# Fused attention and two mixtures on one core: the second mixture's 2 MB loads two steps later, the first long list's tokens one step later, the last gates' operations behind the last denominators

## The chip, the cores and the metric

The kernel runs on 1 core of one Trainium2 chip. A time is the device time of one execution in microseconds (us). Before the change three runs gave 623.2, 625.92 and 627.24 us, so the median is 625.92 us. One more execution was taken by the profiler: 622.31 us, of which the trace covers a span of 620.5 us from the first to the last instruction. All rows below come from that execution, and their start times are us from the span's start.

The engines are named as in the profile: PE is the matmul engine (PEld its weight loads), DVE the vector engine, ACT the scalar engine, POOL the general engine, SP the engine that issues most of the transfers (SPq is its queue).

## The reference

Three layers follow each other, in 32-bit floats.

```
attention: 2 batches x 8 heads, 768 tokens, head width 64; keys and queries are assigned
           to one of 16 clusters of their head, and a query sees the keys of its cluster
           scores = q.k / 8 with a mask; softmax; times v        -> x, 1536 tokens x 512
mixture 1: logits = x@w_gate + log1p(exp(x@w_noise)) * noise     (8 experts)
           top 2 experts of each token, softmax over the two
           out[token] += weight * (relu(x@w1[e]) @ w2[e])        w1 512x1024, w2 1024x512
mixture 2: logits = x@phi (32 slots, 4 per expert)
           slot_input = softmax over tokens(logits).T @ x
           slot_out   = relu(slot_input @ w1[e]) @ w2[e]
           out        = softmax over slots(logits) @ slot_out
```

## The kernel before, in words

**Attention.** Pairs of heads are worked on one after the other; a pair has 12 units of scores, so the table of things to do runs over units, and `LAST` = 84 is the first unit of the last pair. Each half of a pair ends with its denominators (`den`: PE sums, a transpose `dt` and a reciprocal `rd` on DVE) and with `xout`, which writes the tokens' rows `x` and the parts of the gates' logits `gp`.

**Gates.** The first mixture's routing is made in three pieces of 6, 3 and 3 chunks of 128 tokens (`Dispatch.gate`). A piece is a list of some 40 short operations, on DVE mostly (line L690 is the helper that issues them); it has one call of `rank`, which is six small operations on PE (tile `prank`, L736 to L739) that wait for the piece's two-hot matrix `mb`. At the end stand the scatters of 128 rows each into the lists `xg`, on POOL (L757). The list `todo` holds all these operations with the unit from which each may be issued, and `gap(s, n)` takes up to n of them where the kernel's code calls it. So the numbers in `mix`, `lead` and `quota` set where the operations stand between other work on every engine. `LEAD[1]` is how many of the second piece's operations may go from unit 96, ahead of the last denominators; the others go from 99. `lead` says how many are issued around the first call of `M1.first`, `quota` how many before and after `M1.second` in steps 0 to 3. Some names in the rows are reused rooms: the third piece's tiles are cut out of `xr`.

**First mixture.** There are ten lists of tokens (jobs): two short ones of 256 rows (half the tokens of experts 0 and 1), six long ones of 448 down to 384 rows (experts 2 to 7, sorted by size at run time, `perm`), and two short ones again. Each list takes 8 steps, one for each 128 of the 1024 hidden columns: steps 0 to 15 are the first two lists, 16 to 63 the long ones, 64 to 79 the last two. In step s the kernel issues `first(s+1)` (12 matmuls into `ph`, L1054; then H on ACT, L1059, and its remainder on DVE, L1060), `second(s)` (matmuls into `py`, L1094 for short and L1121 for long lists) and the split of weights for step s+3 into a high part (ACT, L952) and a low part (DVE, L959). `load_w(s+5)` loads 512 KB of weights into one of four rooms `wr` (L946, L948), which the low part of step s+1 sets free.

**Tokens of a list.** `load_x(j)` loads a list's rows (`xr`, L975, four transfers) and its weights and row numbers (`mt`, L987, L989) on SP. For the first long list it stands behind `load_perm`, which reads six expert numbers into SP's registers (L938); the step is `LX`. For the other long lists it stands in the second step of the list before. The rows are transposed on DVE (`prep_t`, L1009) from the third step of that list on, copied on ACT (L1016), and the low part is made on DVE or POOL (L1022). A finished long list is turned back by 16 transposes on DVE (L1130), scaled on ACT, and added to the result `x2acc` in DRAM by POOL's indirect transfers (L1144).

**Second mixture.** Its weights come in halves of 2 MB (`M2.load_w`, L1205, tile `v`). Six of them go at the steps in the table `V1`, all on SP's queue, in between the first mixture's loads. They are used in the second mixture only.

What fixes the order is the order of the code: each engine executes its own instructions in the order in which they were issued, and SP its transfers.

Of the kernel before, what the change touches and what calls it, by code (L numbers as in the profile page):

```python
# [52 lines left out]
PH, PL = 1, 1  # L53
JX, JT, JN = 4, (10, 2), 2
SC = -9, -8, -7, -6, -5, -4, -3, -2, -1, 0, 1, 2
LEAD = 1, 16
SP = 1, 2, 3, 4, 6, 8
SL, MX = 1, 94
LT = (8, 9), (6, 6)
# [8 lines left out]

UN = (0,) + (10,) * 9 + (9,) * 4
SLOTS = {0: (0, 0, 2, 2, 1, 2, 2), 9: (0, 2, 1, 1, 2, 1, 2), 10: (0, 2, 1, 2, 1, 2, 2)}  # L70
V1 = 32, 36, 40, 44, 48, 58
TURN = 3, 4, 3, 3, 3, 4, 0, 0
LAST = 12 * (NP - 1)

# [400 lines left out]
class Dispatch:  # L475
# [68 lines left out]
    def gate0(self, n):  # L544
# [6 lines left out]
        def t(name, *shape, dt=F32):  # L551
            if name not in T:
                m = 1
                for x in shape:
                    m *= x
                names = " ".join("abc"[:len(shape)])
                a = g.place(m) if dt is F32 else g.place(m // 2).bitcast(dt)
                T[name] = a.rearrange(f"p ({names}) -> p {names}", **dict(zip("abc", shape)))
            return T[name]
# [7 lines left out]
        PL, PW = (lambda i=i: self.pg[:, 8 * n * i:8 * n * i + 8 * n].rearrange("p (c e) -> p c e", e=E) for i in range(2))  # L567
        M0, M1, V0, V1, TT, SS = (lambda k=k: t(k, n) for k in ("m0", "m1", "v0", "v1", "tt", "ss"))
        MB = lambda: t("mb", n, E, dt=BF16)
# [5 lines left out]
        def op(f, *a, **k):  # L575
            out.append(lambda: f(*[x() if callable(x) else x for x in a], **k))
# [38 lines left out]
        op(TTn, PW, PW, bce(self.iode), op=OP.mult)  # L615
        top(V1, PW)
        op(TTn, oh[1], PW, lambda: bcn(V1()), op=OP.is_equal)
        op(PT, MB, oh[0], oh[1], op=OP.add)
# [879 lines left out]
def body(tc, qk, q2, k2, v2, cent, wgn, noise, w12, phi, v12, out):  # L1498
    nc = tc.nc
    with ExitStack() as ctx:  # L1500
# [152 lines left out]
        for i in range(Dp.NFILL):  # L1653
            at(ends, 2 * (i // 4) + 3, Dp.fill, i)

        LX = 8
        todo = []
        gates = [Dp.gate(q, *x) for q, x in enumerate(((0, 6), (6, 3), (9, 3)))]

        def mix(s, ops, rows, every):  # L1660

            rows = list(rows)
            for i, f in enumerate(ops):
                todo.append((s, f))
                if rows and i % every == every - 1:
                    todo.append((s, rows.pop(0)))
            todo.extend((s, f) for f in rows)
# [8 lines left out]
        n1, n2 = at_rank(a), at_rank(z)  # L1676
        mix(MX, a[:LEAD[0]], [], 1)
        mix(96, a[LEAD[0]:LEAD[1]], [], 1)
        x, y = a[n1 + 1:], z[9:n2]
        turns = a[LEAD[1]:n1] + z[:9] + a[n1:n1 + 1]  # L1680
        while x:
# [4 lines left out]
        mix(99, z[n2:], [], 1)  # L1686
        mix(99, [], gates[2][1], 1)
        half = len(todo) - half
        quota = {0: (19, 9), 1: (9, 0), 2: (14, 14), 3: (14, 14)}
        lead = n1 - LEAD[1] + 1, 4  # L1690

        def gap(s, n):
            while n > 0 and todo and todo[0][0] <= s:
# [126 lines left out]
        for s in range(ns):  # L1820
            j, f = M1.steps[s]
            if 4 + len(SP) <= s + 5 < ns:
                M1.load_w(s + 5)
            if s == LX:
                while todo:
# [46 lines left out]
            if s == X9:  # L1872
                M1.load_x(9)
            if s in V1:
                M2.load_w()
# [78 lines left out]
```

## Time and profile before

| | before |
|---|---|
| runs (us) | 623.2, 625.92, 627.24 |
| profiled execution (us) | 622.31 |
| its span (us) | 620.5 |
| PE busy | 598.1 us, 96% |
| DVE busy | 426.2 us, 69% |
| ACT busy | 323.0 us, 52% |
| POOL busy | 288.3 us, 46% |
| granted PE clock, mean | 0.997 |
| moved by transfers | 139.50 MB, 225 GB/s over the span |

A row of the timeline gives the start, the duration, the engine, the line, the operation, the tiles (written <- read), how many were merged, and in brackets how long the engine was idle just before and what ended that. Shares of busy time are of little use here, since PE is nearly always busy: what matters is where PE has gaps, and which engine or transfer ended each of them.

### The profile page before, as it was taken

What the parts mean: (1) busy time and instruction counts of PE and PEld (TensorE: products, weight loads), DVE (VectorE), ACT (ScalarE), POOL (GpSimd) and SP (SyncE); (2) the same over time, 40 slices, a digit from 0 to 9 for tenths busy, and PEclk for the clock granted to TensorE, in tenths of its full rate; (3) what the DMA queues carried; (4) which work ended last, traced back from release to release, by engine and by line L of the source; (5) the groups of instructions that cost most, each with busy time, mean ns of one, the idle gap of its engine ahead of it and who ended that gap; (6) DMA issues with size and microseconds to landing.
All of it is one profiled execution on the core that took longest, in us unless ns stands there. A gap on an engine that the chain in (4) does not pass through costs nothing. (4 is left out here: it accounts for less than half of the span.)

```text
span 620.5 us, 11580 instructions
## 1 busy us (share of the span) xinstructions
PE 598.1 (96%) x4215; PEld 482.7 (78%) x4215; DVE 426.2 (69%) x854; ACT 323.0 (52%) x470; POOL 288.3 (46%) x266
## 2 busy tenths in 40 slices
PE   8999999999999998999999999999989999988996
PEld 6666767666677766878999999999989988875544
DVE  6875787676776498757455949878675877646633
ACT  5877667676676571545344463545536365533002
POOL 3998778787989851643030250513306034220100
PEclk9999999999999999999999999999989999999999
DMA  8262475552347684897835479798986979988995
GB/s 311 87 233 68 159 277 190 184 188 107 129 173 256 233 242 157 270 246 189 198 102 127 144 205 269 264 295 311 291 187 141 261 234 331 318 282 308 425 396 205
DMA packets 59116, 139.50 MB, mean 225 GB/s; under 512 B 11504, under 2 KB 27056, under 8 KB 57008
## 3 DMA queue, kind: packets, MB, share of 16 engines
q1 hardware_dynamic: 53168, 125.31, 59.9%
q0 software_dynamic: 5888, 13.42, 10.4%
q8 instruction: 34, 0.56, 0.4%
q14 instruction: 26, 0.21, 0.1%
HBM read 108.18 MB, written 28.42 MB: 220 GB/s over the span
## 5 line engine op out<-in xcount | busy, mean ns | idle before, releaser
L959 DVE TENSOR_TENSOR ring<-wr,ring 128x1024 fp32r<-128x1024 f32 (+1 forms) x77 | 98.6, 1281 | 64.6 <-ACT ring L952 64.5
L952 ACT ACTIVATE ring<-wr 128x1024 fp32r<-128x1024 f32 x77 | 81.5, 1059 | 84.9 <-PE py L1121 52.7
L1121 PE MATMUL py<-H,ring 128*128 128x448 f32 (+5 forms) x480 | 100.1, 356 | 3.0 <-DVE H L1060 3.0
L1121 PEld LDWEIGHTS py<-H,ring 128*128 128x128 f32 x480 | 89.2, 190 | 7.2 <-DVE H L1060 4.6
L347 DVE TENSOR_REDUCE mp<-pmx 128x1 f32<-128x512 f32 x96 | 63.6, 683 | 13.3 <-PE pmx L342 12.6
L390 ACT ACTIVATE pts<-psc 128x768 f32<-128x768 f32 x72 | 57.8, 811 | 23.4 <-PE psc L386 20.1
L1059 ACT ACTIVATE H<-ph 128x256 fp32r<-128x256 f32 (+7 forms) x80 | 36.5, 456 | 63.0 <-PE ph L1054 57.3
L1054 PE MATMUL ph<-XS1a,ring 128*128 128x240 f32 (+3 forms) x288 | 68.1, 327 | 0.0
L1094 PE MATMUL py<-ring,H 128*128 128x512 f32 x246 | 63.7, 397 | 1.2 <-DVE H L1060 1.2
L1054 PE MATMUL ph<-XS0a,ring 128*128 128x432 f32 (+3 forms) x252 | 63.0, 332 | 1.2 <-DVE dt L450 1.1
L1144 POOL DMA_INDIRECT x2acc<-y,mdi x20 | 32.8, 1640 | 60.3 <-ACT y L1135 24.8
L1060 DVE SCALAR_TENSOR_TENSOR H<-ph,H 128x256 fp32r<-128x256 f32 (+7 forms) x80 | 41.0, 513 | 18.0 <-ACT H L1059 16.8
L1094 PEld LDWEIGHTS py<-ring,H 128*128 128x128 f32 x246 | 43.9, 188 | 10.2 <-DVE H L1060 2.5
L403 PE MATMUL pav<-pts,vt 128*64 128x384 f32 x288 | 51.7, 492 | 0.0
L423 POOL TENSOR_TENSOR psa<-psa,pts 128x768 f32<-128x768 f32 x27 | 49.7, 1841 | 3.5 <-ACT pts L390 1.9
L1022 POOL TENSOR_TENSOR XS0b<-xr,XS0a 128x512 fp32r<-128x512 f32 (+1 forms) x9 | 14.8, 1646 | 76.4 <-ACT XS0a L1016 76.4
L1054 PEld LDWEIGHTS ph<-XS1a,ring 128*128 128x128 f32 x288 | 48.2, 190 | 2.0 <-DVE ring L959 0.2
L1054 PE MATMUL ph<-XS0b,ring 128*128 128x256 f32 (+3 forms) x192 | 46.7, 316 | 1.3 <-ACT ring L952 0.7
L1054 PE MATMUL ph<-XS1b,ring 128*128 128x240 f32 (+3 forms) x192 | 46.3, 315 | 0.8 <-DVE ring L959 0.8
L1054 PEld LDWEIGHTS ph<-XS0a,ring 128*128 128x128 f32 x252 | 43.3, 189 | 2.8 <-DVE dt L450 1.3
L403 PEld LDWEIGHTS pav<-pts,vt 128*64 128x64 f32 x288 | 19.2, 136 | 23.1 <-issue 21.4
L757 POOL DMA_INDIRECT xg<-x,idx x24 | 25.7, 1073 | 21.7 <-DVE inv L690 15.8
(382 smaller groups left out, 1190.4 us busy)
## 6 DMA issues: line engine op xcount, KB each, us to landing
wr<-in_w SPq DMA_DIRECT2D x80, 512.0 KB
v<-in_v SPq DMA_DIRECT2D x9, 2048.0 KB
xg<-xr SPq DMA_DIRECT2D x14, 516.0 KB
wr<-in_qk SPq DMA_DIRECT2D x8, 768.0 KB
early<-in_q SPq DMA_DIRECT2D x8, 768.0 KB
early<-in_k SPq DMA_DIRECT2D x8, 768.0 KB
x2acc<-xr SPq DMA_DIRECT2D x8, 512.0 KB
vt<-in_v SPq DMA_DIRECT2D x8, 384.0 KB
```

Source lines behind the costliest of these rows:

```text
L347: nc.vector.tensor_reduce(mp[:, 0, col:col + 1], ps, axis=AX.X, op=OP.max)
L390: nc.scalar.activation(pt, ps[:, :, :384], AF.Exp, scale=SCALE)
L403: nc.tensor.matmul(self.avp[p, qh][64 * hh:64 * hh + 64, :384], self.vt[p][:, hh, kc, :], pt[:, hh, :], start=(kc == 0), stop=(kc == 5))
L423: eng.tensor_tensor(s, s, pt.pop((p, t)), op=OP.add)
L952: self.nc.scalar.activation(self.ring[s][0], self.wr[s], AF.Copy)
L959: nc.vector.tensor_tensor(lo[:, :n], wr[:, :n], f32(hi)[:, :n], op=OP.subtract)
L1054: nc.tensor.matmul(ph[:, :u], a[:, 128 * c:128 * c + 128], x[:, c, :u], start=(c == 0 and i == 0), stop=(c == 3 and i == 2))
L1059: nc.scalar.activation(HH[:, :u], ph[:, :u], AF.Relu)
L1060: nc.vector.scalar_tensor_tensor(HL[:, :u], ph[:, :u], 0.0, f32(HH)[:, :u], op0=OP.max, op1=OP.subtract)
L1094: nc.tensor.matmul(py, x, y, start=(f == 0 and i == 0), stop=(f == NF - 1 and i == 2))
L1121: nc.tensor.matmul(py[:, :w], a[:, k], x[:, :w], start=(f == 0 and i == 0), stop=(f == NF - 1 and i == 2))
L1144: st = nc.gpsimd.indirect_dma_start(out=out, out_offset=bass.IndirectOffsetOnAxis(ap=di, axis=0), in_=y, in_offset=None, compute_op=OP.add)
```

## The change

Three edits, all in numbers that set the order.

- `V1`: five of the six 2 MB loads stand two steps later. Those at the first step of a list (32, 40, 48) go to the third (34, 42, 50), and so from ahead of the next list's tokens, which stand in the second step, to behind them. Those at the fifth step (36, 44) go to the seventh (38, 46).
- `LX`: the six reads of expert numbers and the first long list's tokens go from step 8 to step 9, behind one more load of weights.
- `LEAD[1]`, `lead`, `quota`: 4 instead of 15 operations of the second gates' piece stand ahead of the last denominators, and the others are spread over the first steps of the first mixture with other numbers.

```
-LEAD = 1, 16
+LEAD = 1, 5
...
-V1 = 32, 36, 40, 44, 48, 58
+V1 = 34, 38, 42, 46, 50, 58
...
-        LX = 8
+        LX = 9
...
-        quota = {0: (19, 9), 1: (9, 0), 2: (14, 14), 3: (14, 14)}
-        lead = n1 - LEAD[1] + 1, 4
+        quota = {0: (9, 8), 1: (14, 12), 2: (14, 14), 3: (14, 14)}
+        lead = 9, 6
```

**SP's queue around step 48, before.** `v_3783` is a 2 MB half of the second mixture, `xr` and `mt` are the tokens of the last long list, `wr` the weights of steps 52 to 54.

```order
L946 DMA wr<-in_w 128x1024
L1205 DMA v_3783<-in_v 128x4096
L946 ISA
L946 DMA wr<-in_w 128x1024
L975 ISA
L975 DMA xr<-xg 32x12x128
...
L987 DMA mt<-xg 128x3x4
```

**The same place in SP's queue now.**

```order
L946 DMA wr<-in_w 128x1024
L975 ISA
L975 DMA xr<-xg 32x12x128
...
L987 DMA mt<-xg 128x3x4
L946 ISA
L946 DMA wr<-in_w 128x1024
L1205 DMA v_3783<-in_v 128x4096
```

The 2 MB load stood two transfers ahead of the tokens and now stands behind them and one more load of weights. The same holds for the lists that follow steps 32 and 40.

**SP's queue at the first long list, as a difference.** The rows are the last loads for the second short list, then loads of weights, then the reads of the expert numbers (`permi`).

```order
 L975 DMA xr<-xg 32x8x128 x4
 L982 DMA mt<-xg 128x2x4
-L948 DMA wr<-in_w 128x1024 x8
+L948 DMA wr<-in_w 128x1024 x9
 L938 TENSOR_LOAD permi x6
 L975 ISA
```

The weights of step 14, which stood behind the first long list's tokens, are now the ninth load ahead of the reads and of the tokens.

**PE at the last gates, as a difference.** The first row is the last `xout` of attention; the two steps' `ph` that follow are the first mixture's steps 0 and 1; `prank` is the rank of the second piece of gates.

```order
 L464 MATMUL px<-iw,ot 128x160 x3
 L1054 MATMUL ph<-XS0a,ring 128x256 x24
+L1094 MATMUL py<-ring,H 128x512 x6
+L1054 MATMUL ph<-XS0a,ring 128x256 x12
 L736 LDWEIGHTS tri
 L736 MATMUL prank<-mb,tri 128x24
```

The rank stood behind `first(1)` and now stands behind `second(0)` and `first(2)`. The third piece's rank keeps its place behind `first(3)`. On DVE the last `dt`, `rd`, `x` and `gp` now stand ahead of eleven operations of the second piece that stood ahead of them, and the remainders of H for steps 0 to 3 stand further forward among the gates' operations.

## Rows read from the trace of the kernel before

**Rows 1.** Busy time, share and instructions, from the page.

```profile
PE 598.1 (96%) x4215; PEld 482.7 (78%) x4215; DVE 426.2 (69%) x854; ACT 323.0 (52%) x470; POOL 288.3 (46%) x266
```

**Rows 2.** Chain of waits, steps 52 and 53: start, us, what.

```profile
456.20 2.14 PE ph L1054 x12
...
460.71 3.42 PE py L1121 x11
464.14 2.48 PE ph L1054 x12
466.62 2.13 PE py L1121 x12
```

**Rows 3.** Windows on PE: length, PE busy (matmuls), granted clock, DMA share, GB/s.

```profile
450.00:452.00 2.00, 2.00 (x13) 1.00 1.22 181
...
462.00:463.00 1.00, 1.00 (x5) 0.50 0.23 33
...
465.00:466.00 1.00, 1.00 (x8) 1.00 0.00 0
```

**Rows 4.** Timeline of DVE, the transposes of the two last long lists' tokens.

```profile
420.00 0.71 DVE L1009 STREAM_TRANSPOSE xr<-xr 128x512 f32<-128x512 f32 x1 [1.26 <-DMA mt<-xg]
...
457.58 0.71 DVE L1009 STREAM_TRANSPOSE xr<-xr 128x512 f32<-128x512 f32 x1 [3.34 <-DMA xr<-xg]
```

**Rows 5.** Timeline of SP's queue, tokens of three long lists and one 2 MB load.

```profile
332.83 2.18 SPq L975 DMA_DIRECT2D xr<-xg  x4
...
406.95 6.21 SPq L975 DMA_DIRECT2D xr<-xg  x4
...
437.44 0.45 SPq L1205 DMA_DIRECT2D v<-in_v  x1
...
442.83 5.91 SPq L975 DMA_DIRECT2D xr<-xg  x4
```

**Rows 6.** Timeline of PE, the two smaller gaps of the long lists.

```profile
423.14 2.25 PE L1121 MATMUL py<-H,ring 128*128 128x400 f32 x11 [0.29 <-DVE H L1060]
...
432.51 2.26 PE L1121 MATMUL py<-H,ring 128*128 128x400 f32 x11 [0.47 <-DVE H L1060]
```

**Rows 7.** One line's instructions: shortest, median, longest ns, first and last start.

```profile
L938 SPq TENSOR_LOAD <-permi x6: 263/279/586, 264.4 to 266.2; - x6
```

**Rows 8.** Timeline of SP's queue behind those reads.

```profile
267.13 2.13 SPq L975 DMA_DIRECT2D xr<-xg  x4
...
272.62 1.00 SPq L948 DMA_DIRECT2D wr<-in_w  x2
```

**Rows 9.** Timeline of DVE, ACT and PE, steps 7 to 14.

```profile
265.29 1.21 DVE L959 TENSOR_TENSOR ring<-wr,ring 128x1024 fp32r<-128x1024 f32 x1
...
277.45 1.06 ACT L952 ACTIVATE ring<-wr 128x1024 fp32r<-128x1024 f32 x1 [3.39 <-DMA wr<-in_w]
...
278.56 0.50 PE L1054 MATMUL ph<-XS0b,ring 128*128 128x256 f32 x2 [0.71 <-ACT ring L952]
...
286.04 1.20 PE L1094 MATMUL py<-ring,H 128*128 128x512 f32 x4 [0.48 <-DVE H L1060]
```

**Rows 10.** Timeline of PE at the last gates, steps 0 to 2.

```profile
237.03 1.70 PE L1054 MATMUL ph<-XS0a,ring 128*128 128x256 f32 x12 [1.08 <-DVE dt L450]
239.58 0.19 PE L736 MATMUL prank<-mb,tri 128*128 128x24 bf16 x1 [0.85 <-DVE mb L690]
...
240.91 1.19 PE L1094 MATMUL py<-ring,H 128*128 128x512 f32 x4 [0.50 <-DVE H L1060]
...
246.82 0.19 PE L736 MATMUL prank<-xr,tri 128*128 128x24 bf16 x1 [0.48 <-DVE xr L690]
```

**Rows 11.** Timeline of DVE in the same stretch.

```profile
236.70 0.28 DVE L450 STREAM_TRANSPOSE dt<-pden 128x96 f32<-128x96 f32 x1
...
241.80 0.42 DVE L1060 SCALAR_TENSOR_TENSOR H<-ph,H 128x256 fp32r<-128x256 f32 x1 [0.82 <-ACT H L1059]
...
245.82 0.42 DVE L1060 SCALAR_TENSOR_TENSOR H<-ph,H 128x256 fp32r<-128x256 f32 x1 [0.40 <-ACT H L1059]
```

## The prediction

> **What bounds the kernel now.** The page's busy line comes first: PE is busy for 96% of the span [rows 1], so only its gaps and its clock are to be won. The chain of waits, read in order of time, shows steps of the long lists that are nothing but PE, `ph` and `py` in turn at 2.14 and 2.13 us, with one break [rows 2]: a `ph` ends at 458.34 (456.20 + 2.14), and the next `py` starts at 460.71. A `py` and a `ph` should take 4.27 us; this pair ends at 466.62, after 8.28 us. So 4.01 us were lost: 2.37 of waiting, and 1.64 because the matmuls behind it were slow. The windows tell why: the granted clock was 0.50 (1.2 GHz) at 462 to 463 and 1.00 (2.4 GHz) again at 465 [rows 3].
>
> The timeline of DVE names what PE waited for. At 457.58 DVE had been idle for 3.34 us for the last list's tokens, and the transposes and the remainder H that PE wanted were queued behind that transpose; at 420.00 there was a smaller wait of 1.26 us [rows 4]. SP's queue tells why the tokens were late: four token transfers take 2.18 us to issue where no 2 MB load stands ahead, and 6.21 and 5.91 us where one does [rows 5]. The third list with one ahead looks alike. Two small gaps of PE, 0.29 and 0.47 us, follow the wait at 420 [rows 6].
>
> Two more groups of gaps lie earlier: at steps 13 to 15, where weights land late [rows 9], and at the last gates, where PE waits for DVE [rows 10].
>
> **Part 1, the 2 MB loads.** Five move, none is added. Three (steps 32, 40, 48) leave the place ahead of the tokens. The tokens' issue then takes about 2.2 us, that is 3.7 us less at 442.83 and 4.0 us less at 406.95 [rows 5]. DVE waited 3.34 and 1.26 us [rows 4], so both waits are covered, the first with only 0.4 us to spare by issue alone; the 2 MB that no longer share the engines with the tokens come on top. If DVE does not stop, PE's break goes with the clock's drop (4.01) and so do the two gaps (0.29 + 0.47): **4.8 us**. The lower bound is 0, if the tokens are late for another reason; I take the upper end because the issue time, the nearest row, names the 2 MB load.
>
> What is late next? Each moved load now stands straight ahead of a load of weights. So did those at steps 36 and 44 before, and ACT waited for no weights in the long lists; weights are loaded five steps ahead and wanted two steps on. If that cover were gone, each of the five would cost up to the 3.7 us by which one held the tokens, less the cover. The load of step 46 comes within three steps of the last list's tokens, 12.8 us (3 x 4.27) ahead; it held the queue for 3.7 to 4.0 us in the rows, so it is out of the way. The last one (step 58) stays. All are used in the second mixture only, which hides the two steps.
>
> **Part 2, the first long list's tokens one step later.** On SP the weights of step 14 go ahead of six reads and the tokens. Their room is free when DVE ends at 266.50 (265.29 + 1.21) [rows 9], and they were issued at 272.62 [rows 8]: 6.1 us earlier. They landed when ACT could go on at 277.45, and ACT had wanted them 3.39 us before, at 274.06 [rows 9]. So this wait goes. The reads start at 264.4 and the tokens at 267.13 [rows 7, 8], 2.7 us, so the tokens now start at about 266.5 + 0.3 + 2.7 = 269.5, 2.4 us later, and the weights of step 15, the second of the row at 272.62 [rows 8], at about 275. Weights took 4.83 us from 272.62 to landing at 277.45; at that pace those of step 15 land at about 280, where ACT would want them a step after 274.06, at about 277 (a short list's step is a `ph` of 1.70 and a `py` of six where four take 1.19, partly overlapped [rows 10]): up to 3 us of the 3.39 could come back one step on. PE's gaps in that stretch are 0.71 and 0.48 us [rows 9]. Bounds: 1.2 us gained if all of it goes, 0 if it only moves. That pace was measured with the tokens in front and a second load of weights behind; now the tokens alone are in front, so I take a value nearer the upper end: **0.8 us**.
>
> **Part 3, the gates.** The operations are the same; only their order changes. The last `dt` at 236.70 goes ahead of eleven operations [rows 11], which frees the PSUM room of `first(1)`, so PE's 1.08 us goes. The second piece's rank goes behind `second(0)` and `first(2)`, so the 0.85 us goes; and H of step 0 is made earlier, so the 0.50 us goes mostly [rows 10]. PE reached the third piece's rank at 246.34 (246.82 - 0.48) and will reach it some 2.4 us earlier, at 243.9. But that rank waits for DVE, which has all of its work still. DVE's idle times there are 0.82 and 0.40 us, both for ACT's H [rows 11]. The 0.40 goes, for H will be ready; the 0.82 stays in another form, since the third piece's own operations wait for ACT's exponentials where an H used to fill in. So the rank comes 0.4 us earlier, at 246.4, and PE waits 2.5 us in one piece where it waited 2.91 in four. Gain **0.4 us**; bounds +1.2 (both waits) and -0.4 (a second wait like the 0.40). The scatters on POOL start with the second piece's end, which moves by no more than that.
>
> **Sum.** 4.8 + 0.8 + 0.4 = 6.0 us off the profiled execution's own 622.31 us: 616.3. The median of the three runs, 625.92, stands 3.6 us above that execution; with the same saving it becomes **619.9 us**, which is 1.0% less, so the case lies on the bound of 1% (6.3 us), about what a measurement of this kernel can tell from no change.
>
> **The rivals.**
>
> *More than the sum.* The runs stand 3.6 us above the profiled execution with the same work. If this is more of the waits for transfers that Part 1 takes away, the median comes to 616.3 as well. For it: the waits depend on other traffic, and one drop of the clock weighs 1.6 us. Against it: nothing shows where the runs lost it. Chance 0.13.
>
> *The clock at the gates.* PE's waiting is gathered into one piece of 2.5 us ahead of the third rank, and a wait of 2.37 us was followed by half clock [rows 2, 3]. The same 1.64 us would be lost behind 246.4: 6.0 - 1.6 = 4.4, so 617.9 for the profiled execution, 621.5 for the median. Against it: 2.43 us of waiting between 236 and 241, in three pieces [rows 10], left the clock whole. The Trainium skill, "TensorE: Matmul & The Clock Gate", Part 1, says that half rate is where PE stands when idle and that sustained activity has to release it; the trace agrees at 462 us, and by that rule this edit, which joins four short waits into one, is for the worse. Chance 0.22.
>
> *The 2 MB load is not what held the tokens.* The tokens move in small pieces: at 450 to 452 the engines were full (share 1.22) at only 181 GB/s [rows 3], and POOL's additions to `x2acc` go at the same time. If the tokens are slow by themselves, Part 1 gives nothing and 1.2 us are left: 621.1, and 624.7 for the median. For it: full engines; against it: 2.18 against 5.91 us [rows 5]. The Trainium skill, "DMA: Bandwidth & Descriptors", Specifications, gives a fabric ceiling of 435 GB/s and about 0.6 us to the first byte for SP's path: by an estimate from that page 2 MB take 4.8 + 0.6 us, and a load issued at 437.44 is gone at 442.9, as the tokens' issue begins, which would make this rival's 621.1. The trace disagrees, with 5.91 us of issue from 442.83 on. Chance 0.14.
>
> *The first long list's tokens come late.* They start at 269.5, and DVE reaches their transpose at about 276.3 (274.06 + 1.06 for ACT's high part + 1.21 for a low part [rows 9]), with the low parts of weights and H of the next steps queued behind it. The last list's tokens took 14.7 us from the start of their issue to 457.58 [rows 4, 5]; the same here means 284.2. DVE stops for 7.9 us, PE for about 1 us less (what H of the steps before lets it do), and the clock takes 1.6 more: 8.5 lost against 5.2 won elsewhere, 3.3 us slower, 625.6 for the profiled execution and 629.2 for the median. It costs from a landing past about 277 on, and makes the whole slower from about 281 on. Against it: no 2 MB load is near, and 2.13 us of issue [rows 8]. Chance 0.06.
>
> **Numbers.** My forecast has 0.45. Range: from 615.0 (the case above it, with the spread of a median) to 625.0 (the tokens' rival); about 0.15 lies outside. Faster by over 1%: 0.13 from the first rival, half of 0.45, a quarter of 0.22: 0.41. Slower by over 1% needs the last rival with a later landing still: 0.05. Within 1%: 0.54.
>
> **What would show it.** Part 1: token issues of about 2.2 us at all long lists, no idle time of DVE ahead of a token transpose, no clock of 0.5 between 290 and 510, `py` and `ph` without a break; wrong if ACT waits for weights behind a moved load. Part 2: ACT's wait of 3.39 us gone and one of at most 3 us a step later. Part 3: one gap of 2 to 3 us ahead of the third rank, the rank near 246.4; a clock of 0.5 behind it means the second rival.

## The result, and the profile after

The changed kernel took **617.42 us** in the median of four runs (616.91 to 618.04), the kernel before, run beside it, 626.58 us in four (623.2 to 629.16). The ratio is 0.9857, with a 95% interval of 0.9808 to 0.9907: 1.4% faster. The profiled execution took 617.21 us, against 622.31 us before, so profiled executions differ by 5.1 us and medians by 9.2 us. The forecast had 616.3 us and 619.9 us for the two: the profile came out 0.9 us above it, the median 2.5 us below. Where the 4 us between the two differences came from is the main thing that the experiments had to settle.

The page of the changed kernel, busy time of each engine; it answers to [rows 1]:

```profile
span 615.4 us, 11576 instructions
...
PE 595.6 (97%) x4215; PEld 482.7 (78%) x4215; DVE 424.1 (69%) x854; ACT 322.8 (52%) x470; POOL 291.3 (47%) x266
```

SP's queue, the tokens of the three long lists that had a 2 MB load ahead of them; they answer to [rows 5]:

```profile
370.72 1.96 SPq L975 DMA_DIRECT2D xr<-xg  x4
...
406.46 2.93 SPq L975 DMA_DIRECT2D xr<-xg  x4
...
441.09 2.90 SPq L975 DMA_DIRECT2D xr<-xg  x4
...
446.44 0.43 SPq L1205 DMA_DIRECT2D v<-in_v  x1
```

They issue in 2 to 3 us where they took 6.21 and 5.91. On DVE the transposes that wait for them, which answer to [rows 4]:

```profile
418.25 0.70 DVE L1009 STREAM_TRANSPOSE xr<-xr 128x512 f32<-128x512 f32 x1
...
452.44 0.70 DVE L1009 STREAM_TRANSPOSE xr<-xr 128x512 f32<-128x512 f32 x1
```

Nothing stands in brackets behind them: DVE was not idle. The long lists have no gap of PE left, so [rows 2] and [rows 6] have no counterpart. The windows (length, PE busy, PEld, DVE, ACT, POOL, granted clock, DMA share, GB/s) give the stretch of [rows 3], and two others that the text comes back to:

```profile
247.00:249.00 2.00, 2.00 (x14) 1.77 (x13) 1.70 (x10) 0.00 (x0) 1.39 (x3) 1.00 0.41 155
...
460.00:465.00 5.00, 5.00 (x30) 5.00 (x30) 4.86 (x7) 2.80 (x5) 2.25 (x2) 1.00 0.38 130
558.00:560.00 2.00, 1.64 (x9) 1.31 (x10) 0.92 (x3) 0.00 (x0) 0.00 (x0) 0.70 1.02 381
560.00:562.00 2.00, 2.00 (x12) 1.56 (x16) 0.69 (x1) 0.70 (x2) 0.00 (x0) 0.50 1.05 309
```

The clock is whole (2.4 GHz) at 460 to 465, where it was 0.50 at 462 to 463 before [rows 3], but it is 0.50 (1.2 GHz) at 560 to 562, in the second mixture.

SP, ACT and PE at the first long list's tokens; they answer to [rows 8, 9]:

```profile
269.94 2.00 SPq L975 DMA_DIRECT2D xr<-xg  x4
...
274.17 0.52 SPq L948 DMA_DIRECT2D wr<-in_w  x1
```

```profile
279.59 1.06 ACT L952 ACTIVATE ring<-wr 128x1024 fp32r<-128x1024 f32 x1 [2.87 <-DMA wr<-in_w]
```

ACT's wait of 3.39 us for weights went from step 14 to step 15 and is 2.87 us there.

PE at the gates, which answers to [rows 10], and in the second mixture:

```profile
246.52 0.19 PE L736 MATMUL prank<-xr,tri 128*128 128x24 bf16 x1 [2.61 <-DVE xr L690]
246.64 1.65 PE L1094 MATMUL py<-ring,H 128*128 128x512 f32 x6
...
558.36 1.60 PE L1290 MATMUL pt<-ident,XS1ab 128*128 128x128 f32 x8 [1.05 <-DMA XS1ab<-x2acc]
559.89 1.97 PE L1290 MATMUL pt<-ident,ringb 128*128 128x128 f32 x8
```

The four small gaps ahead of the third rank have become one of 2.61 us, and the `py` behind it has its usual 1.65 us, so the clock stayed whole here. The two `pt` at 558 take 1.60 and 1.97 us where eight such matmuls take 1.09: that is the half clock of the windows.

**A ruler for all profiles.** H of a step starts on ACT (L1059) when its `ph` is done, so its start is a mark in every profile. In the changed kernel:

```profile
273.52 0.38 ACT L1059 ACTIVATE H<-ph 128x256 fp32r<-128x256 f32 x1 [0.37 <-PE ph L1054]
...
289.73 0.54 ACT L1059 ACTIVATE H<-ph 128x448 fp32r<-128x448 f32 x1 [1.81 <-PE ph L1054]
...
502.38 0.37 ACT L1059 ACTIVATE H<-ph 128x240 fp32r<-128x240 f32 x1 [0.21 <-PE ph L1054]
```

These are steps 12, 16 and 64; before they stood at 273.68, 289.76 and 508.14. With the start of `first(0)` (before 234.25, now 234.90) and the span's end, four stretches can be compared whatever came earlier: "gates" from `first(0)` to step 12, "12-16", "lists" from 16 to 64, and "rest" from 64 to the end. The table has every profile of this study; the last four were taken on another chip. "Drop" says where PE's clock was at 0.50 for some 2 us or more beside or behind a wait: G behind the third rank, S at a stop between 252 and 262 that only the other chip shows, L where the last long list's tokens are transposed (steps 52 to 54), T at the start of the second mixture.

| profile | gates | 12-16 | lists | rest | drop |
|---|---|---|---|---|---|
| before | 39.43 | 16.08 | 218.38 | 112.36 | L |
| before again | 39.41 | 15.84 | 219.45 | 113.70 | L T |
| tokens only | 39.78 | 16.53 | 219.62 | 115.70 | L T |
| gates only | 38.70 | 17.41 | 222.18 | 115.57 | L T |
| loads only | 39.97 | 15.88 | 212.66 | 116.35 | T |
| changed | 38.62 | 16.21 | 212.65 | 113.02 | T |
| changed again | 40.83 | 15.71 | 212.65 | 112.17 | G |
| loads behind tokens | 40.75 | 15.94 | 212.77 | 117.73 | G T |
| first load of a list only | 40.57 | 16.11 | 212.66 | 112.28 | G |
| two loads ahead | 39.02 | 15.94 | 230.84 | 113.99 | L T, and at 390 to 396 |
| reads early (other chip) | 43.22 | 15.66 | 212.65 | 116.62 | G T |
| third rank later (other chip) | 41.84 | 16.21 | 212.66 | 116.22 | S T |
| both together (other chip) | 42.43 | 16.13 | 212.66 | 114.85 | S T |
| second weights later (other chip) | 45.99 | 16.04 | 212.66 | 117.06 | G S T |

### The profile page after: what moved, and what is told of

Same layout as the page of the kernel before. It is cut to its first block, busy times and chain, and to the rows that moved or that the text cites. A ratio compares the mean times of both kernels' runs of the same rounds, so it can differ in the third digit from the quotient of the medians.

```text
span 615.4 us, 11576 instructions
## 1 busy us (share of the span) xinstructions
PE 595.6 (97%) x4215; PEld 482.7 (78%) x4215; DVE 424.1 (69%) x854; ACT 322.8 (52%) x470; POOL 291.3 (47%) x266
## 5 line engine op out<-in xcount | busy, mean ns | idle before, releaser
L959 DVE TENSOR_TENSOR ring<-wr,ring 128x1024 fp32r<-128x1024 f32 (+1 forms) x77 | 94.0, 1222 | 63.3 <-ACT ring L952 62.8
L1121 PE MATMUL py<-H,ring 128*128 128x448 f32 (+5 forms) x480 | 97.8, 352 | 0.0
L1059 ACT ACTIVATE H<-ph 128x256 fp32r<-128x256 f32 (+7 forms) x80 | 36.5, 456 | 65.7 <-PE ph L1054 59.8
L1022 POOL TENSOR_TENSOR XS0b<-xr,XS0a 128x512 fp32r<-128x512 f32 (+1 forms) x9 | 17.0, 1884 | 69.2 <-ACT XS0a L1016 51.3
L1022 POOL TENSOR_TENSOR XS1b<-xr,XS1a 128x512 fp32r<-128x512 f32 (+1 forms) x6 | 11.4, 1904 | 54.0 <-ACT XS1a L1016 54.0
```

The lines of the kernel that those rows point to most:

```text
L959: nc.vector.tensor_tensor(lo[:, :n], wr[:, :n], f32(hi)[:, :n], op=OP.subtract)
L1059: nc.scalar.activation(HH[:, :u], ph[:, :u], AF.Relu)
L1121: nc.tensor.matmul(py[:, :w], a[:, k], x[:, :w], start=(f == 0 and i == 0), stop=(f == NF - 1 and i == 2))
```

## The experiments

Each was run in five rounds beside the kernel before. The first four shared a chip, as did the next four (the same one); the last four ran on another.

### The parts alone

**The 2 MB loads alone** (the kernel before with this):

```
-V1 = 32, 36, 40, 44, 48, 58
+V1 = 34, 38, 42, 46, 50, 58
```

> The kernel before with the five 2 MB loads moved and nothing else. Theory A (the place of the 2 MB loads carries the change, in the profiled execution and in the runs): 5.5 to 6 us less span than the 620.5 of the profiled execution before, no idle time of DVE ahead of the transposes of the tokens of lists 5 to 7, no half clock near 461, and nearly the whole difference of the medians, 8 to 9 us, with runs that agree within about 1 us. Theory B (the three parts share it): 4 to 5 us of the medians' difference. Theory C (gates and tokens carry it): 0 to 2 us.

**The tokens' step alone:**

```
-        LX = 8
+        LX = 9
```

> The kernel before with the first long list's tokens one step later and nothing else. Theory A and my reading of the trace after: the wait of ACT for weights only moves from step 14 to step 15, so 0 us, within 1; ACT idle 2 to 3 us for the weights of step 15 at about 277. Theory B: 1 to 2 us faster. Theory C: 2 us or more faster.

**The gates' order alone:**

```
-LEAD = 1, 16
+LEAD = 1, 5
...
-        quota = {0: (19, 9), 1: (9, 0), 2: (14, 14), 3: (14, 14)}
-        lead = n1 - LEAD[1] + 1, 4
+        quota = {0: (9, 8), 1: (14, 12), 2: (14, 14), 3: (14, 14)}
+        lead = 9, 6
```

> The kernel before with the gates' three numbers changed and nothing else. Theory A: 0.5 to 1 us faster, one PE gap of about 2.6 us ahead of the third rank in place of four short ones; a half clock behind it would turn the gain into a loss of about 1 us. Theory B: 1 to 2 us. Theory C: over 3 us.

**The kernel before once more,** with no edit, for the spread of its profile and of its runs:

> The kernel before, unchanged, to see in a second trace where its executions differ (623.2 to 629.16 in four runs, against 622.31 in the profiled one; 616.91 to 618.04 after). Theory A: the step times of lists 5 to 7 differ between the two traces of this kernel, by longer waits of DVE for tokens and by one or two more stretches at half clock, and the rest of the span agrees within 1 us. Rival: the difference lies in attention or in the second mixture, and the steps of the long lists agree within 1 us.

| | median (us) | runs | ratio to before | 95% interval |
|---|---|---|---|---|
| loads only | 620.11 | 615.8 to 620.64 | 0.9886 | 0.9847 to 0.9924 |
| tokens only | 625.70 | 620.48 to 629.17 | 0.9988 | 0.9955 to 1.0021 |
| gates only | 626.77 | 620.72 to 629.42 | 0.9994 | 0.9965 to 1.0023 |
| before again | 624.69 | 622.61 to 629.09 | 0.9985 | 0.9959 to 1.0011 |
| before, beside them | 626.18 | 621.61 to 631.1 | | |

Only the loads move the time; of the tokens' step and the gates' order no effect shows outside the intervals. Theory A had the loads' place right and three figures wrong: the loads alone took 6.1 us off the median (626.18 - 620.11) and not 8 to 9, their profiled span is 618.7 us and not 614.5 to 615, and their runs spread over 4.8 us. The lists took 212.66 us as forecast; the span was lost in the rest, 116.35 us. For the kernel before, run again, the theory had the rest within 1 us: it is 1.3 us longer, the lists 1.1 us, each with half clock. So there are two places by which its executions differ.

The profiles say what the loads do. All four with the loads in their old place (the first of them [rows 2]) have PE stopped at the last long list's tokens, for 2.21, 2.60, 3.18 and 3.34 us, with slow matmuls behind. The longest, from the kernel with the gates' order alone, on PE, DVE and SP:

```profile
463.58 3.96 PE L1121 MATMUL py<-H,ring 128*128 128x392 f32 x11 [3.34 <-DVE H L1060]
```

```profile
421.73 0.71 DVE L1009 STREAM_TRANSPOSE xr<-xr 128x512 f32<-128x512 f32 x1 [2.79 <-DMA xr<-xg]
...
460.45 0.71 DVE L1009 STREAM_TRANSPOSE xr<-xr 128x512 f32<-128x512 f32 x1 [4.46 <-DMA xr<-xg]
```

```profile
407.08 7.17 SPq L975 DMA_DIRECT2D xr<-xg  x4
444.56 6.44 SPq L975 DMA_DIRECT2D xr<-xg  x4
```

The edit of that kernel lies 180 us ahead of this place and touches nothing here, so we take the difference for one between executions; two profiles of the very same kernel differ by 1.1 us in the lists. In the table the lists take 218.38, 219.45, 219.62 and 222.18 us with the old loads and 212.65 to 212.77 us with the moved ones. **So the profiled execution on which the prediction rests was the mildest of four.** Their mean is 219.9 us: the loads are worth 7.3 us on the average of these profiles, and not the 5.7 us of that execution.

### The suspected cost doubled

**Two 2 MB loads ahead of the tokens of each of the three lists:**

```
-V1 = 32, 36, 40, 44, 48, 58
+V1 = 31, 32, 39, 40, 47, 48
```

The sixth load comes ten steps earlier here, into a room in which the first mixture still turns finished rows (`wide`), so part of its rows is overwritten; no instruction's time hangs on their values.

> The kernel before with two 2 MB loads ahead of each long list's tokens (one in the same step, one in the step before it), where it had one. If a 2 MB load holds the tokens' issue by 3.7 us and the DMA engines are the narrow place, the second one holds them by up to 5.7 us more (the 4.01 us lost and about 1.7 us): DVE's waits of 1.26 and 3.34 us become 4 to 8 us in each of the three lists, each with PE stopped and half clock behind it, 8 to 15 us slower than before (634 to 642). If the queue has room again 4.27 us after the earlier load (a step), the second one costs little: 0 to 3 us slower (626 to 629).

It took 636.3 us (634.4 to 639.44), ratio 1.0193 (1.0143 to 1.0242), within the forecast of the theory. DVE's waits were 5.09, 3.89 and 1.86 us, for 4 to 8 forecast, and PE stopped for 4.02, 2.90 and 4.83 us; the clock fell at the first and the last stop and stayed whole at the second. SP's queue and DVE:

```profile
370.87 9.96 SPq L975 DMA_DIRECT2D xr<-xg  x4
...
413.27 8.37 SPq L975 DMA_DIRECT2D xr<-xg  x4
...
458.46 4.86 SPq L975 DMA_DIRECT2D xr<-xg  x4
```

```profile
388.17 0.71 DVE L1009 STREAM_TRANSPOSE xr<-xr 128x512 f32<-128x512 f32 x1 [5.09 <-DMA mt<-xg]
...
428.98 0.71 DVE L1009 STREAM_TRANSPOSE xr<-xr 128x512 f32<-128x512 f32 x1 [3.89 <-DMA ident_i<-in_phi]
...
470.99 0.71 DVE L1009 STREAM_TRANSPOSE xr<-xr 128x512 f32<-128x512 f32 x1 [1.86 <-DMA xr<-xg]
```

Four token transfers take about 2 us to issue with no load ahead, 5.0 to 7.2 with one and 8 to 10 with two, where both stand within two steps (at 365.14 and 360.85 for the first row). For the last list the first of the pair went 15 us ahead of the tokens, and their issue took 4.86 us. The lists took 230.84 us, 12.5 more than in the profile of before. The names behind two of these waits (`mt`, `ident_i`) are not the tokens: the transposes wait for several semaphores, and the profile names one.

### What of the place matters

Both variants were run with the change itself once more, for comparison on their chip.

> The changed kernel once more, on the chip of its variants. Theory A (the tokens behind a 2 MB load, and the half clock that follows each late token, made both the loss and the spread): 616.5 to 618.5 us, ratio 0.984 to 0.990. Theory B (the first result's 9 us were partly its chip): 619.5 to 621.5, by the 5.1 us that the two profiled executions differ.

**Each moved load one step earlier, directly behind the tokens:**

```
-V1 = 34, 38, 42, 46, 50, 58
+V1 = 33, 37, 41, 45, 49, 58
```

> The change with each moved 2 MB load one step earlier: in the tokens' own step of a long list, but behind the tokens' issue, where it has three steps or more to the next tokens. Order theory: what holds the tokens is only what is queued ahead of them on SP, so the tokens issue in 2 to 3 us and the time is that of the change within 1 us (616.5 to 619). Distance theory: the 2 MB share the DMA engines with the tokens that are landing, so the tokens come late although they were issued first: DVE waits 1 to 3 us ahead of a token transpose in the last list, PE stops and the clock falls to 0.50 behind it, 2 to 4 us slower than the change (619.5 to 622).

**Only the loads that stood ahead of tokens:**

```
-V1 = 34, 38, 42, 46, 50, 58
+V1 = 34, 36, 42, 44, 50, 58
```

> The change with only the three 2 MB loads moved that stood ahead of a list's tokens (steps 34, 42, 50); the other two stay at steps 36 and 44. If only the load ahead of the tokens counts, this is the change's time within 1 us. If the moves of the other two matter (8 us more room to the next list's tokens for the change's 46, or two 2 MB loads two steps apart here), there is a wait for tokens or weights near 400 to 450 us and 1 to 4 us more than the change.

| | median (us) | runs | ratio to before | 95% interval |
|---|---|---|---|---|
| changed again | 616.57 | 615.61 to 618.61 | 0.988 | 0.9833 to 0.9926 |
| loads behind tokens | 620.24 | 615.72 to 622.99 | 0.9916 | 0.9883 to 0.9949 |
| first load of a list only | 620.35 | 616.38 to 622.47 | 0.9928 | 0.9897 to 0.9959 |
| before, beside them | 624.24 | 620.91 to 628.62 | | |

The stretch that the loads are in has one answer: 212.77 and 212.66 us against 212.65, with token issues of 2.0 to 3.4 us and no wait ahead of a token transpose. Order is what counts there, not distance, and the loads of steps 36 and 44 need not have moved. Directly behind one of these loads ACT waited 2.14 us for weights once (at 425.97, with the loads behind the tokens), and the lists grew by no more than 0.12 us. But the medians are 3.7 us above the change's (the intervals overlap). The distance theory's 619.5 to 622 holds the 620.24, but the wait that it names did not come; the order theory has the stretch right and the time wrong. The profile with the loads behind the tokens shows that its own loss lies in the rest (117.73 us against 112.17). PE and the clock there:

```profile
560.90 1.97 PE L1290 MATMUL pt<-ident,XS1ab 128*128 128x128 f32 x8 [2.51 <-DMA XS1ab<-x2acc]
563.02 1.94 PE L1290 MATMUL pt<-ident,ringb 128*128 128x128 f32 x8 [0.15 <-DMA ringb<-x2acc]
```

```profile
560.00:562.00 2.00, 1.10 (x5) 1.10 (x6) 0.00 (x0) 0.00 (x0) 0.00 (x0) 0.54 0.91 334
```

PE waits there for the last sums to be read back from `x2acc`, which wait for POOL's last additions. That wait is 0.84 us in one profile and 3.15 in another, and it is in kernels with old and moved loads alike. The `pi` matmuls just ahead of it start 53.85 to 54.07 us behind H of step 64 in all ten profiles of the table's upper part, so what their rests differ by lies behind that point. The traces also show what made it long. In the loads alone, the tokens alone and the gates alone (2.75, 3.15 and 2.27 us) POOL's last addition but one had to wait until an earlier read of `x2acc` had landed, and both last additions went out over 1 us later, behind H of step 64, than in the changed kernel. The row of the changed kernel, then that of the loads alone:

```profile
547.51 1.56 POOL L1144 DMA_INDIRECT x2acc<-y,mdi  x1 [14.40 <-ACT y L1163]
```

```profile
549.02 1.56 POOL L1144 DMA_INDIRECT x2acc<-y,mdi  x1 [15.94 <-DMA XS1ab<-x2acc]
```

With the loads behind the tokens the additions went out in time, but the last one took 5.95 us from its issue until the read behind it could go, for 4.64 us in the changed kernel. No experiment changed this chain.

The profile of the other variant (rest 112.28) has no drop there, while its runs have low clocks: of its 12 runs 9 record a mean clock of 0.994 or less, of the 12 with loads behind tokens 8, of the loads alone 3 of 6, of the change's ten in both sittings 2. A mean clock does not say where a run was slow, so that the runs spread by this drop is likely but not shown. Why the change as a whole should meet it more seldom than its loads alone is **open**.

### The two gaps that were left

These ran on a chip on which the kernel before took 631.56 us (627.13 to 636.27). In all four profiles PE, DVE and ACT stopped together between 252 and 262, which no other profile shows; so their sums say little, and the single places are compared. The change itself was not run on that chip.

**The reads of expert numbers early, the tokens at step 9:**

```
-            if s == LX:
+            if s == 8:
                 while todo:
                     gap(1000, 1000)
                 M1.load_perm()
+            if s == LX:
                 M1.load_x(2)
```

> The change with the six reads of the permutation back at step 8 and only the first long list's tokens at step 9, so that the reads pass while SP waits for room. If the wait of 2.87 us that ACT still has (for the weights of step 15, queued behind reads and tokens) comes from the 2.7 us of the reads, the tokens are issued near 267.3 instead of 269.9, that wait falls below 0.7 us, and step 16 starts about 1 us earlier against step 12 (12.5 us for 13.5): 1 us less than the change, 615.5 to 617.5. If the engines are what is full there, the tokens and weights land no earlier and nothing is gained: step 12 to 16 in 13.3 to 13.6 us.

(The expectation counts to the start of step 16's `ph`, the table to its H, 2.7 us later; by its count this run has 12.97 us, the change 13.51 and, run again, 13.03.) It took 623.83 us, ratio 0.9886 (0.9842 to 0.993). The theory falls. ACT's wait is still there:

```profile
283.31 1.06 ACT L952 ACTIVATE ring<-wr 128x1024 fp32r<-128x1024 f32 x1 [2.35 <-DMA wr<-in_w]
```

and on SP:

```profile
264.27 7.19 SPq L948 DMA_DIRECT2D wr<-in_w  x3
271.77 2.88 SPq L975 DMA_DIRECT2D xr<-xg  x4
...
275.55 2.42 SPq L989 DMA_DIRECT2D mt<-xg  x2
278.08 0.52 SPq L948 DMA_DIRECT2D wr<-in_w  x1
```

H of step 12 started at 277.77 here, so the tokens were issued 6.0 us ahead of it, and 3.6 us ahead (273.52 - 269.94) in the changed kernel: 2.4 us earlier, as meant. But the weights of step 15 started 0.3 us behind that H (278.08), against 0.65 us (274.17) in the change: the token and `mt` transfers took 2.88 and 2.42 us to issue, for 2.00 and 1.31. What the reads gave back, the transfers behind them took. From step 12 to 16 it took 15.66 us, against 15.71 and 16.21 us for the change.

**The third piece's rank behind two more pieces of mixture work:**

```
-        quota = {0: (9, 8), 1: (14, 12), 2: (14, 14), 3: (14, 14)}
+        quota = {0: (9, 8), 1: (12, 9), 2: (7, 4), 3: (14, 14)}
```

> The change with the third piece's rank behind the second(2) and the first(4) instead of ahead of them (DVE's work the same). If PE's one gap of 2.61 us ahead of that rank is only a matter of order, it falls below 0.5 us and step 12 starts about 2 us earlier against first(0) (36.6 us for 38.6): 2 us less than the change, 614.5 to 616.5. If the stretch is set by DVE and ACT, the gap comes back in other places up to step 12 and less than 0.5 us is won. If the gathering that hangs on the rank becomes late, later lists lose it again.

It took 623.13 us, ratio 0.988 (0.9833 to 0.9927). PE at the rank, with no bracket behind it:

```profile
245.02 1.58 PE L1054 MATMUL ph<-XS0a,more 128*128 128x256 f32 x12
246.45 0.19 PE L736 MATMUL prank<-xr,tri 128*128 128x24 bf16 x1
```

and ACT, H of steps 4 and 5:

```profile
246.64 0.38 ACT L1059 ACTIVATE H<-ph 128x256 fp32r<-128x256 f32 x1 [1.15 <-issue]
...
254.73 0.38 ACT L1059 ACTIVATE H<-ph 128x256 fp32r<-128x256 f32 x1 [6.24 <-remote]
```

The gap of 2.6 us and the half clock behind it are gone at this place (the clock falls to 0.50 at 255 to 258 instead), and H of step 4 comes at 246.64, where the kernel with the reads early, on the same chip, has it at 250.77: 4.1 us won at this place. One step on, ACT's H waits 6.24 us for something that the profile calls "remote". From `first(0)` to step 12 it took 41.84 us, against 43.22 with the reads early, so 1.4 us of the 4.1 are left. On the first chip this was not tried.

**Both together:**

> The change with both edits, reads early and third rank later. If both theories of their places hold, 3 us less than the change: 613 to 615.5, ratio 0.980 to 0.985 to the kernel before. If the moved waits are set by other engines: the change's time.

622.6 us (622.27 to 625.25), ratio 0.9878 (0.9835 to 0.9921): the lowest median of the four, within the others' intervals, and not shown to be better than the change (0.9857 and 0.988, on the first chip).

**1 MB of the second mixture's weights behind the last reads of the sums:**

```
-LOADS = {..., -4: ("b3",), -3: ("c0", "c1")}
+LOADS = {..., -4: ("b3",)}
...
-        for i in range(2, 4):
+        for i in range(4):
             M2.part(c, 4, i)
```

> The change with 1 MB of the second mixture's weights (two of the last four wr loads) issued behind the last reads of the summed tokens instead of ahead of them. Theory: what still spreads the runs (615.6 to 618.6) is PE's wait at 558 for those tokens, 0.84 to 1.05 us in the change and up to 2.75 with half clock behind it; the additions that they wait for share the engines with these loads. With 1 MB less ahead of them (2.4 us at the 419 GB/s of 565 to 570) the wait falls below 0.8 us in every profile, no half clock follows, and all runs lie within 1.5 us, near 615.5. Rival: the wait is set by the chain of additions and reads alone, and the spread stays. Second rival: the 1 MB is then late for the second mixture, a gap opens at 570 to 600 and the time is 1 to 3 us above the change.

625.35 us, ratio 0.9909 (0.9871 to 0.9946). The theory falls: the wait was 2.67 us, for less than 0.8 forecast and 2.74 to 3.19 in the other three profiles of this chip, and a second one came behind it. PE, and the last addition but one on POOL:

```profile
566.83 1.09 PE L1290 MATMUL pt<-ident,XS1ab 128*128 128x128 f32 x8 [2.67 <-DMA XS1ab<-x2acc]
568.93 1.94 PE L1290 MATMUL pt<-ident,ringb 128*128 128x128 f32 x8 [1.00 <-DMA ringb<-x2acc]
```

```profile
555.78 1.56 POOL L1144 DMA_INDIRECT x2acc<-y,mdi  x1 [15.81 <-DMA XS1ab<-x2acc]
```

So this 1 MB does not set it. The addition waits here, as in the loads alone, for the earlier read of `XS1ab`, issued at 547.29; the edit left what stands ahead of that read as it was. What makes that read land late stays open.

## Why the prediction was right or wrong

**Part 1, the 2 MB loads: mechanism right, size too small.** Forecast 4.8 us; the lists took 218.38 us before and 212.65 after, so 5.73 us in the profiled execution. The sum counted only the gaps that stood in brackets (4.01 + 0.29 + 0.47). By the starts of H, steps 45 and 46 lost 1.25 us where the two brackets gave 0.76, and step 38, behind the third list with a load ahead, lost 0.57 us. The prediction said of that list that it looks alike, and counted nothing for it. DVE and PE there, before and then in the changed kernel:

```profile
383.52 0.71 DVE L1009 STREAM_TRANSPOSE xr<-xr 128x512 f32<-128x512 f32 x1 [0.56 <-DMA mt<-xg]
...
391.22 0.58 DVE L1060 SCALAR_TENSOR_TENSOR H<-ph,H 128x408 fp32r<-128x408 f32 x1
...
391.44 2.73 PE L1121 MATMUL py<-H,ring 128*128 128x408 f32 x12
```

```profile
389.62 0.58 DVE L1060 SCALAR_TENSOR_TENSOR H<-ph,H 128x408 fp32r<-128x408 f32 x1
...
391.40 2.44 PE L1121 MATMUL py<-H,ring 128*128 128x408 f32 x12
```

The `py` has no bracket, but before it had begun 0.36 us ahead of the end of its H's remainder (391.22 + 0.58 = 391.80), and it took 0.29 us longer; now that remainder is done at 390.20. DVE's wait of 0.56 us is a part of its delay; its split of weights in between also took longer (2.13 us for 1.22), and what lengthened that the rows do not tell. Against the mean of four profiles Part 1 is 7.3 us. All that was named to look for came: issues of 2 to 3 us, no idle DVE, no clock of 0.5 and no gap in the long lists, no wait for weights behind a moved load.

**Part 2, the tokens' step: 0.8 us forecast, nothing measured.** Steps 12 to 16 took 16.08 us before and 16.21 after; alone, 16.53 against 15.84 in the second profile of before. In the upper part of the table the five profiles with the tokens at step 8 have 15.84 to 17.41 us, the five with step 9 15.71 to 16.53. The lower bound was right, and the reason given for a value near the upper end failed: "the tokens alone are in front" of the weights of step 15. They took 5.42 us from their issue to ACT's start (274.17 to 279.59), not less than the 4.83 us of step 14's, and the wait moved one step (2.87 us for 3.39).

**Part 3, the gates: 0.4 us forecast, 0.8 in the profile, none on average.** The order moved as predicted, into one gap of 2.61 us. That the rank came at 246.52, for 246.4 forecast, is chance: `first(0)` started 0.65 us later than before, and counted from there the rank came 0.95 us earlier (11.62 for 12.57). From `first(0)` to step 12 it takes 38.62 and 38.70 us where the clock stays whole, some 0.8 less than the 39.5 us of the five profiles with the old order (39.02 to 39.97). But of the seven profiles that have this gap (2.61 to 2.64 us) five show half clock behind it. The change, run again:

```profile
245.98 0.19 PE L736 MATMUL prank<-xr,tri 128*128 128x24 bf16 x1 [2.64 <-DVE xr L690]
246.09 2.12 PE L1094 MATMUL py<-ring,H 128*128 128x512 f32 x6
```

```profile
247.00:249.00 2.00, 2.00 (x9) 1.71 (x8) 1.18 (x6) 0.00 (x0) 1.70 (x2) 0.51 0.68 262
```

There the stretch takes 40.57 to 40.83 us on the first chip, 1.2 us more than the 39.5. So the rival of the clock at the gates was true more often than not, at 2.1 us (40.7 - 38.6) instead of 1.64, and it went unseen in the total because Part 1 gave more. My argument against it, that three smaller waits had left the clock whole, was no evidence on one of 2.6 us in one piece. That half rate is where PE stands when idle (the Trainium skill, "TensorE: Matmul & The Clock Gate", Part 1) agrees with these five; the two profiles with 2.61 and 2.62 us and a whole clock do not show it.

**The profiled time.** 617.21 us against 616.3 looks closer than the parts were. The lists gave 5.7 us for 4.8, the gates 0.8 for 0.4, steps 12 to 16 lost 0.1 where 0.8 was forecast as won, and two stretches that the forecast took as fixed cost 1.3 us: `first(0)` started 0.65 us later, and the rest took 0.66 us longer, with half clock behind the wait at 558. That these nearly cancel is luck.

**The median.** The forecast took the profile's saving over to the median. What failed is that step: it took the profiled execution for a typical one with a fixed 3.6 us on top. Of the four profiles with the old loads it has the shortest lists and the shortest rest; the other three are on average 2.0 us longer in the lists (220.4 for 218.38) and 2.6 us in the rest (115.0 for 112.36). For the lists the rival "more than the sum" (616.3) was right, and its counter-argument "nothing shows where the runs lost it" the weak one: with the old loads they vary by 3.8 us over four profiles, with the moved ones by 0.1 us over nine on two chips. For the rest it was not: the loads alone left it long (116.35 us). The medians fell by 9.2 and 7.7 us (624.24 - 616.57); by the means of four profiles and of two, 7.3 us of it come from the lists and 1.7 us from the rest (114.3 - 112.6). That the change shortens the rest is not shown by two profiles, and why it should stays open.

**The rival that the 2 MB load did not hold the tokens** is disproved from both sides: without it issues and waits go, with two of them the issues grow at two lists of three, and so do the waits. By the fabric ceiling of the Trainium skill, "DMA: Bandwidth & Descriptors", Specifications, an estimate has a 2 MB load gone just as the tokens' issue began (442.9 and 442.83), provided that it has the engines to itself. The rows decide against that estimate: the issue took 5.91 us. **The slower rival** (tokens landing past 281) did not come: DVE's first token transpose started at 278.26 after 1.09 us of waiting:

```profile
278.26 1.11 DVE L1009 STREAM_TRANSPOSE xr<-xr 128x896 f32<-128x896 f32 x1 [1.09 <-DMA xr<-xg]
```

## What to carry to other kernels

A load that nobody needs soon belongs behind the transfers that somebody waits for, in issue order on its queue; how far behind did not matter for the lists here. When the runs stand several us above the profiled execution, look in the profile for a stretch that hangs on transfers and ends in half clock: its cost in one profile may be the mildest. A wait that only moves to the next step is worth nothing, so follow the queue past the place where the wait is removed.

## What the runs showed of the hardware

- The issue time of four token transfers on SP grew with the 2 MB loads just ahead: 2.0 to 3.5 us for none, 4.9 to 7.2 for one, 8.4 to 10.0 for two.
- The length of one wait does not decide whether PE's clock falls: it fell behind 1.05 us (the change at 558) and 1.32 us (before again), and stayed whole behind 1.29 us (before, at 564), 2.61 and 2.62 us (the change and the gates alone, at the third rank) and 2.90 us (two loads ahead, at 432).
- With the same program the second chip was slower (631.56 against 624.24 and 626.18 us), and its profiles have PE, DVE and ACT stopped together around 252 to 262, ACT for up to 7.34 us, ended by what the profile calls "remote". Its cause is not shown.
